# Batch 0 pools q and k on chip from its local tiles, local attention without zero padding, the token rounds cut anew, and the priorities of the order replaced

## The chip, the cores and the metric

The kernel runs on one core of a Trainium2 chip. The metric is the device time of one execution in microseconds. The core has a matrix engine (TensorE, PE in the profile; its weight loads are shown apart as PEld), a vector engine (VectorE, DVE), a scalar engine (ScalarE, ACT), GpSimd (POOL) and SyncE (SP), which here only issues DMAs. Matmul results go to PSUM, which has eight banks of 2 KB per partition.

## The reference

Inputs: q, k, v of shape (4, 8, 576, 64) in fp32, and the weights of two MLPs, w_in (512 x 2048) and w_out (2048 x 512) each, which numpy draws in fp64. The three steps are:

```
q_d, k_d, v_d = mean over each 4 tokens           # 576 -> 144
out_up   = repeat(softmax(q_d k_d^T / 8) v_d, 4)  # "global" attention
out_local = softmax(mask(q k^T / 8)) v            # mask: |i - j| < 4
x = out_up + out_local                            # 2304 tokens x 512
h = x @ moe_w_in;  x = (h * cos(h)) @ moe_w_out
h = x @ moe2_w_in; out = relu(h)**2 @ moe2_w_out
```

## The kernel before

**Tokens and rounds.** The 2304 tokens (4 batches of 576) go through attention and MLP 1 in five rounds, `ROUNDS` (L40): 512, 256, 512, 512, 512 tokens. Weights and activations of the MLPs are split in two fp32r halves, high and low, so each product is three matmuls (`mm3`, L717 to L720). In a round, for each of 16 slices f of the hidden dimension, `mlp_h` makes 128 hidden rows in a PSUM bank with the tag `ps`, ACT and DVE form h cos(h) and its halves, and `mlp_o` adds to four accumulators (tags acc0 to acc3). In round 0 the weights are also converted from fp64 (`convert`, L296 to L308, DVE) and split (L274 on ACT, L277 on DVE); `w_out` goes to DRAM in halves and is loaded again in later rounds. MLP 2 then runs in three blocks of 768 tokens, with seven products for eight (`big_h`, `big_g`, `big_o`), once MLP 1's output is in DRAM.

**Attention units.** For each batch there are four global units (`unit_g`, one pair of heads each, over 144 pooled tokens) and five local units (`unit_l`, tiles of 116 tokens, all eight heads). A round can start when the units that cover its tokens are done (`need`, L1199); the units of the next round are emitted among the work of the current one. Batch 0's units for round 0 are the prologue. Their outputs meet in `xr`, a ring of 640 tokens, from which `split_x` takes the halves xh and xl that `mlp_h` reads.

**A local unit.** The keys of two heads lie in a tile `kz` of 128 partitions in which each head's other 64 partitions are zero, set once by GpSimd (L1251), so that one matmul with 128 rows (q of two heads) and 128 columns gives both heads' scores (L630). A tile has two halves t of 58 queries, which go to output partitions 0 to 57 and 64 to 121. Before them one bf16 matmul of 512 columns writes the mask (L624). Scores of all eight heads fill one bank. `softmax` takes the maximum on DVE (L484); for the first four units (`EXP_SUM`) ACT then takes the exponential group by group with its sum (L498), for the others DVE subtracts (L487), ACT takes one exponential (L492) and DVE sums (L506); DVE divides (L511, L520). PE transposes (L644), ACT copies the two heads into the two partition halves of the zero-padded `pz` (two copies of 64 partitions, L648), PE multiplies with v (L668: 8 matmuls of 128 rows and 116 columns, par choosing the output half), and DVE adds the global part `up_sb` on the way into xr (L694).

**A global unit.** Scores from `qd_sb` (padded per head) and `kd_sb` (L551), the same softmax with ACT's sums, transposes (L567), copies (L570), values with `vd_sb` (L585), and ACT's repeated copy to `up_sb` (L591).

**Pooling.** For batches 1 to 3, GpSimd issues DMAs that add the four phases of q, k, v into `qn_sb`, `kd_sb`, `vd_sb`. For batch 0, q and k are loaded whole a second time (L359), PE sums their phases by identity matmuls (L369), ACT copies (L373, L377), and DVE adds pooled v (L403). Each local tile has its own loads of q, k and v (L441, L445, L448).

**The order.** Every piece is an `op` with an engine, a cost and a key, a due time made of its round and slice. `Plan.order` runs a list schedule over costs and buffer counts: each engine takes what can start first, and among what can start within 0.02 us the smallest key. To the key an entry of the table `OFF` (L53) is added, by the name of the operation and the stage (`STG`) in which its key lies. The resulting order is the program's; on the chip each engine goes through its own part of it, waiting for semaphores. Tags in `IN_TURN` get their buffers in the order of emission. The tag `ps` has four banks. Before the first `mlp_o`, tiny matmuls of zeros (L1240, "idle") fill PE's planned gaps.

Of the kernel before, what the change touches and what calls it, by code (L numbers as in the profile page):

```python
# [7 lines left out]
F32 = mybir.dt.float32  # L8
F32R = mybir.dt.float32r
I32 = mybir.dt.int32  # L10
# [12 lines left out]
QT = 58  # L23
# [10 lines left out]
NORM = 0  # L34
NORM_L = 0
ADD_PE = 0
# [3 lines left out]
ROUNDS = [(0, 512), (512, 256), (768, 512), (1280, 512), (1792, 512)]  # L40
# [16 lines left out]
class Plan:  # L57


    RATE = {"SP": 1.24, "POOL": 2.07}  # L60
    LAT = {"PE": 0.15, "ACT": 0.15, "DVE": 0.15, "SP": 0.0, "POOL": 0.0}

    IN_TURN = ("rawi", "rawo", "w2", "p", "pt", "q", "v", "t", "w1")
# [161 lines left out]
@with_exitstack  # L225
def body(ctx: ExitStack, tc: tile.TileContext, qb, kw, vw, q0, k0, qp, kp, vp, wi, wo, masks, ident, out_t):
# [6 lines left out]
    ATT = ("q", "v", "p", "pt", "mx", "sm")  # L233
# [10 lines left out]
    id16 = const.tile([128, 128], BF16, name="id16")  # L244
    mask16 = const.tile([128, 3, KT], BF16, name="mask16")
    kz = [att.tile([128, 2, 2, PR, KT], F32, name=f"kz{i}") for i in range(2)]
    pz = [att.tile([128, PR, 2, 2, QT], F32, name=f"pz{i}") for i in range(2)]
# [103 lines left out]
    def load_pooled(b, key, after=None):  # L351
        some = [("kd", kd_sb, kp), ("qn", qn_sb, qp), ("vd", vd_sb, vp)]
        if b == 0:
            for c in range(KD):
                for nm, tmp, src, tok in (
                    ("k", xr[:, :, 0:S], k0, [("xr", x) for x in range(XR // 64)]), ("q", up_sb, q0, [("up", x) for x in range(KD)])
                ):
                    def ld(tmp=tmp, src=src, c=c):
                        nc.sync.dma_start(out=tmp[:, c], in_=src[:, c])  # L359

                    op("SP", 0.82, key + c, ld, w=[(nm + "0", c)])

                for nm in ("q", "k"):
                    tile_, src = ("ps", "pool", nm, c), (up_sb[:, c] if nm == "q" else xr[:, c, 0:S])

                    def sums(tile_=tile_, src=src):
                        ps, t = new(tile_, [128, SD], space=PSUM), src.rearrange("p (r g) -> p r g", r=4)
                        for r in range(4):
                            nc.tensor.matmul(ps, id_sb, t[:, r], start=r == 0, stop=r == 3)  # L369

                    def put(nm=nm, tile_=tile_, c=c):
                        if nm == "k":
                            nc.scalar.activation(out=kd_sb[:, c], in_=T[tile_], func=AF.Copy)  # L373
                            return
                        for hh in range(2):
                            pp = slice(64 * hh, 64 * hh + 64)
                            nc.scalar.activation(  # L377
                                out=qd_sb[pp, c, :, hh, :], in_=T[tile_][pp].rearrange("p (t i) -> p t i", i=48),
                                func=AF.Copy,
                            )  # L380

                    op("PE", 1.0, key + c, sums, r=[(nm + "0", c), ("id",)], w=[tile_], new=[tile_])
                    op("ACT", act(SD, 0.05) * (2 if nm == "q" else 1), key + c, put, r=[tile_], w=[(nm + "d", c)])
            for c in range(XR // 64):
                plan.readers[("xr", c)] = sum((plan.writer[("kd", x)] for x in range(KD)), [])
            for c in range(KD):
                plan.readers[("up", c)] = sum((plan.writer[("qd", x)] for x in range(KD)), [])
# [12 lines left out]
            for r in range(1, 4):  # L400
                def add_v(r=r):
                    a = T["w1", "v0", 0][:, 0] if r == 1 else vd_sb
                    nc.vector.tensor_tensor(out=vd_sb, in0=a, in1=T["w1", "v0", r // 2][:, r % 2], op=OP.add)  # L403

                op(
                    "DVE", 1.15, key + 2.5 + 0.5 * r, add_v,
                    r=[("v0", r), ("w1", "v0", r // 2)] + ([("v0", 0)] if r == 1 else []), w=[("vd",)],
                )
            some = []
        else:  # L410
            T_gate = ("gate", b)
            op(
                "POOL", 0.0, key - 0.1, lambda: nc.gpsimd.tensor_copy(out=gate, in_=T[after][0:1, 0:1].bitcast(F32)), r=[after],
                w=[T_gate],
            )
        before = ("gate", b)
        for nm, dst, src in some:
            for r in range(4):
                how = OP.bypass if r == 0 else OP.add
                op(  # L420
                    "POOL", 0.82, key, lambda dst=dst, src=src, r=r, how=how: nc.gpsimd.dma_start(
                        out=dst, in_=src[b, r], accum_op=how), r=[("gate", b)] + ([before] if r == 0 else []),
                    w=([(nm, c) for c in range(KD)] if nm == "kd" else [(nm,)]) + [("pool", b, nm)],
                )
            before = ("pool", b, nm)

    def home(b, d):

        if b == 0 and d in (2, 3):
            return ("ki", "q", d), ("e", "v", d), d  # L430
        return ("q", b, d), ("v", b, d), 0 if (b, d) == (0, 4) else (b * ND + d) % 2

    def keys(kt):
        return kz[kt] if kt < 2 else T["w1", "kz"][:, kt - 2]

    def load_local(b, d, key):
        q, v, kt = home(b, d)
        more = [("w1", "kz")] if kt > 1 else []

        def lq():  # L440
            nc.sync.dma_start(out=new(q, [128, 2, PR, QT]), in_=qb[b, d])  # L441

        def lk(hh):
            pp = slice(64 * hh, 64 * hh + 64)
            nc.sync.dma_start(out=keys(kt)[pp, hh], in_=kw[b, d, pp])  # L445

        def lv():
            nc.sync.dma_start(out=new(v, [128, 2, PR, D]), in_=vw[b, d])  # L448

        if kt == 2:  # L450
            def f_z(i, hh):
                if i == hh == 0:
                    new(("w1", "kz"), [128, 2, 2, 2, PR, KT])
                nc.gpsimd.memset(T["w1", "kz"][64 - 64 * hh:128 - 64 * hh, i, hh], 0.0)

            for i in range(2):
# [929 lines left out]
```

## Time and profile before

| | |
|---|---|
| median of 3 runs | 933.02 us (931.62 to 935.36) |
| profiled execution, span | 930.2 us (the profile gives no other time of it) |
| PE busy | 902.9 us, 97% |
| PE weight loads | 778.6 us, 84% |
| DVE busy | 620.8 us, 67% |
| ACT busy | 428.6 us, 46% |
| POOL busy | 36.1 us, 4% |
| DMA | 204.08 MB, mean 219 GB/s |

The table is part 1 and part 3 of the profile's page. Busy PE time counts from a matmul's start to its modelled end, and matmuls overlap in the pipeline, so 97% says that PE rarely stands idle, not that it runs at its peak. Time that a matmul really takes from the engine is read from the starts of neighbours in the timeline.

### The profile page before, as it was taken

The page shows a single profiled execution, that of the slowest core. Times are in us where ns is not written, and L with a number is a line of the kernel's source. Part 1 is how long each engine was busy: PE and PEld are TensorE (multiplying, and loading weights), DVE is VectorE, ACT ScalarE, POOL GpSimd, SP SyncE. Part 2 cuts the span into 40 slices and gives each one's busy share as a digit, 9 for nine tenths or more (in the row PEclk, how much of TensorE's full clock was granted, in tenths as well). Part 3 has the DMA queues.
Part 4 walks back from the last instruction along what each step waited for, and adds up shares of the span by engine and source line. Part 5 has one row for each costly group of instructions (what it writes and reads, how often), then busy time and mean ns, then how long its engine had stood idle before and what let it go on. Part 6 is the DMA issues. An engine that isn't in the chain of part 4 may idle for free.

```text
span 930.2 us, 14600 instructions
## 1 busy us (share of the span) xinstructions
PE 902.9 (97%) x5456; PEld 778.6 (84%) x5456; DVE 620.8 (67%) x1081; ACT 428.6 (46%) x881; POOL 36.1 (4%) x53
## 2 busy tenths in 40 slices
PE   8899979999899999999999989999999999999998
PEld 8788667898688877888888878998899899999997
DVE  2799999736835359766886789878945453644452
ACT  4966678748656476555675433223311111121111
POOL 2001110110120000000000000000000000000000
PEclk9999999999999999999999999999999999999999
DMA  8848975888756255675888677867776565666643
GB/s 232 283 165 255 300 227 190 258 245 245 207 106 175 84 172 192 246 267 202 282 324 271 238 256 267 302 221 269 229 261 196 177 188 179 209 211 198 182 147 114
DMA packets 79447, 204.08 MB, mean 219 GB/s; under 512 B 9232, under 2 KB 14096, under 8 KB 79376
## 3 DMA queue, kind: packets, MB, share of 16 engines
q1 hardware_dynamic: 75152, 192.51, 62.0%
q0 software_dynamic: 4224, 10.62, 6.2%
q8 instruction: 44, 0.72, 0.3%
q14 instruction: 27, 0.22, 0.1%
HBM read 162.20 MB, written 40.89 MB: 218 GB/s over the span
## 4 chain that ended last, share of the span: by engine, by line
PE 76%; DVE 13%; DMA 6%; ACT 2%; issue 2%; SPq 0%; DVEq 0%
PE acc L718 10%; PE acc L720 10%; PE acc L719 10%; PE pp L718 6%; PE ps L718 6%; PE ps L719 5%; PE ps L720 5%; PE pp L719 5%; PE pp L720 5%; PE acx L1160 2%; PE acx L1158 2%; PE acx L1159 2%; DMA rawo<-in_wo_dram 2%; PE ps L630 2%; DVE wa L303 1%
## 5 line engine op out<-in xcount | busy, mean ns | idle before, releaser
L718 PE MATMUL ps<-xh,w 128*128 128x512 f32 (+1 forms) x320 | 120.5, 377 | 2.5 <-DVE t L758 2.3
L718 PE MATMUL acc<-gh,w 128*128 128x512 f32 (+1 forms) x320 | 120.7, 377 | 1.3 <-ACT w L274 0.6
L720 PE MATMUL acc<-gh,w 128*128 128x512 f32 (+1 forms) x320 | 118.3, 370 | 0.9 <-DVE w L277 0.8
L719 PE MATMUL ps<-xl,w 128*128 128x512 f32 (+1 forms) x320 | 118.1, 369 | 1.1 <-DVE xl L277 1.1
L720 PE MATMUL ps<-xh,w 128*128 128x512 f32 (+1 forms) x320 | 118.2, 369 | 0.5 <-DVE w L277 0.3
L719 PE MATMUL acc<-gl,w 128*128 128x512 f32 (+1 forms) x320 | 118.1, 369 | 0.0
L758 DVE TENSOR_TENSOR t<-t,ps 128x512 f32<-128x512 f32 (+1 forms) x80 | 50.6, 634 | 43.5 <-ACT t L755 43.3
L1090 DVE TENSOR_TENSOR c<-ua,pp 128x384 f32<-128x384 f32 x96 | 52.9, 552 | 34.8 <-PE pp L720 33.2
L277 DVE TENSOR_TENSOR gl<-t,gh 128x512 fp32r<-128x512 f32 (+1 forms) x80 | 50.4, 634 | 34.6 <-ACT gh L274 34.4
L718 PEld LDWEIGHTS ps<-xh,w 128*128 128x128 f32 x320 | 60.3, 188 | 15.2 <-issue 3.0
L718 PEld LDWEIGHTS acc<-gh,w 128*128 128x128 f32 x320 | 60.2, 188 | 13.9 <-issue 1.8
L1128 ACT ACTIVATE xh<-c 128x768 fp32r<-128x768 f32 x32 | 27.1, 846 | 95.5 <-PE acc L720 91.2
L720 PEld LDWEIGHTS acc<-gh,w 128*128 128x128 f32 x320 | 60.3, 188 | 12.7 <-DVE w L277 2.7
L720 PEld LDWEIGHTS ps<-xh,w 128*128 128x128 f32 x320 | 60.3, 188 | 12.0 <-DVE w L277 2.0
L719 PEld LDWEIGHTS ps<-xl,w 128*128 128x128 f32 x320 | 60.3, 189 | 10.9 <-DVE xl L277 1.6
L719 PEld LDWEIGHTS acc<-gl,w 128*128 128x128 f32 x320 | 60.3, 189 | 9.5 <-DVE gl L277 0.5
L1131 DVE TENSOR_TENSOR xl<-c,xh 128x768 fp32r<-128x768 f32 x32 | 30.6, 957 | 56.4 <-ACT xh L1128 56.1
L746 ACT ACTIVATE ki<-ps 128x512 int32<-128x512 f32 (+1 forms) x80 | 44.0, 551 | 49.7 <-PE ps L720 36.8
L274 ACT ACTIVATE gh<-t 128x512 fp32r<-128x512 f32 (+1 forms) x80 | 46.2, 582 | 33.0 <-PE acc L720 23.3
L750 DVE SCALAR_TENSOR_TENSOR t<-ki,ps 128x512 f32<-128x512 int32 (+1 forms) x80 | 50.3, 631 | 16.6 <-ACT ki L746 15.6
L763 ACT ACTIVATE t<-t 128x512 f32<-128x512 f32 (+1 forms) x80 | 46.6, 584 | 26.0 <-DVE t L750 25.3
L1097 ACT ACTIVATE ua<-pp 128x384 f32<-128x384 f32 x24 | 11.7, 489 | 95.5 <-PE pp L720 95.4
(194 smaller groups left out, 2126.8 us busy)
## 6 DMA issues: line engine op xcount, KB each, us to landing
w<-w_dram SPq DMA_DIRECT2D x96, 512.0 KB, 3.4
gh<-w_dram SPq DMA_DIRECT2D x77, 256.0 KB, 2.9
gl<-w_dram SPq DMA_DIRECT2D x77, 256.0 KB, 3.1
rawi<-in_wi_dram SPq DMA_DIRECT2D x32, 512.0 KB, 5.5
rawo<-in_wo_dram SPq DMA_DIRECT2D x32, 512.0 KB, 5.1
w_dram<-w SPq DMA_DIRECT2D x32, 512.0 KB, 4.3
w_dram<-rawo SPq DMA_DIRECT2D x24, 512.0 KB, 4.4
kz<-in_kw_dram SPq DMA_DIRECT2D x36, 128.0 KB, 4.3
```

What stands on the lines that cost most here:

```text
L274: nc.scalar.activation(out=hi(), in_=src(), func=AF.Copy)
L277: nc.vector.tensor_tensor(out=lo(), in0=src(), in1=hi().bitcast(F32), op=OP.subtract)
L718: nc.tensor.matmul(ps, w_hi, r_hi, start=first, stop=False)
L719: nc.tensor.matmul(ps, w_hi, r_lo, start=False, stop=False)
L720: nc.tensor.matmul(ps, w_lo, r_hi, start=False, stop=last)
L746: nc.scalar.activation(out=tt(ki), in_=tt(hp), func=AF.Copy, scale=1.0 / TWO_PI)
L750: nc.vector.scalar_tensor_tensor(out=tt(t), in0=tt(ki), scalar=-TWO_PI, in1=tt(hp), op0=OP.mult, op1=OP.add)
L758: nc.vector.tensor_tensor(out=tt(t), in0=tt(t), in1=tt(hp), op=OP.mult)
L763: "ACT", act(n), key + 0.2, lambda: nc.scalar.activation(out=tt(t), in_=tt(t), func=AF.Abs), w=[t]
L1090: nc.vector.tensor_tensor(out=out(), in0=a(), in1=ps(), op=OP.subtract if sub else OP.add)
L1128: nc.scalar.activation(out=gpart(0, R, f), in_=T[t], func=AF.Copy)
L1131: nc.vector.tensor_tensor(out=gpart(1, R, f), in0=T[t], in1=gpart(0, R, f).bitcast(F32), op=OP.subtract)
```

## The change

- **Local first.** For batch 0 the units are emitted as five local and then four global ones, and round 0 needs all of them. The local output is copied into xr by ACT; the global part is then scaled and added in xr by DVE, two instructions per two heads' pairs.
- **Pooling of batch 0.** The second load of q and k, PE's sums and ACT's copies of them are gone. DVE sums each four tokens of q and k from the local tile (`f_pool`, two reductions per tile); ACT spreads the pooled q. Pooled v is summed by PE (four matmuls of 512 columns for each of two halves), copied by ACT.
- **Local units without padding.** One array `qkv` in DRAM holds a tile's q, k and v; one DMA per tile (two for batch 0, q and k ahead of v) brings them. `kz` and `pz` and their zeroing are gone. Scores are 16 matmuls of 64 rows, 58 outputs and 64 columns: each head's 64 partitions (hh) by each half t. The two heads' results go to two banks. The mask is four bf16 matmuls of 64 rows and 256 columns. Values are 16 matmuls of 64 rows and 58 columns, into two banks. The softmax takes maximum and subtraction per bank; the weights are copied in one instruction of 128 partitions into a `pt` buffer.
- **Global units.** Two units share one product with v and one copy.
- **Constants.** The 16-bit identity and mask come ready-made in one load.
- **Rounds and priorities.** `ROUNDS` becomes 512, 384, 448, 448, 512. The planner's costs of the local products become 0.75 and 0.52 (before 1.25 and 0.95), and `OFF` is replaced by a shorter table.

```diff
+HOMES = ((0, 4),)
+S_PE = 0.75
+PV_PE = 0.52
...
-ROUNDS = [(0, 512), (512, 256), (768, 512), (1280, 512), (1792, 512)]
+ROUNDS = [(0, 512), (512, 384), (896, 448), (1344, 448), (1792, 512)]
...
-        "q": 2, "v": 2, "rawi": 2, "rawo": 2, "wm": 1, "wa": 2, "w2": 3, "p": 3, "pt": 2, "t": 2, "ki": 2,
+        "qkv": 4, "rawi": 2, "rawo": 2, "wm": 1, "wa": 2, "w2": 3, "p": 3, "pt": 2, "t": 2, "ki": 2,
...
+                    for r in range(4):
+                        nc.tensor.matmul(
+                            ps, id_sb[0:SD // 2, 0:SD // 2], T["w1", "v0", r // 2][:, r % 2, kh], start=r == 0, stop=r == 3
+                        )
...
     def load_local(b, d, key):
+        if b:
+            op("SP", 2.08, key, lambda: ld(0, NQ + NK + NV), w=[x, ("v", b, d)], new=[x])
+            return
+        op("SP", 1.36, key, lambda: ld(0, NQ + NK), w=[x], new=[x])
+        op("SP", 0.75, key + 0.5, lambda: ld(NQ + NK, NQ + NK + NV), r=[x], w=[("v", b, d)])
+        n = min(DT, S - DT * d) // 4
+        for nm, dst, lo, m in (("q", qn_sb, 0, DT), ("k", kd_sb, NQ, DT + 6)):
+            def f_pool(dst=dst, lo=lo, m=m, at=3 if nm == "k" else 0):
+                src = T[x][:, lo:lo + PR * m].rearrange("p (r n) -> p r n", r=PR)[:, :, at:at + 4 * n]
+                nc.vector.tensor_reduce(
+                    out=dst[:, :, DT // 4 * d:DT // 4 * d + n], in_=src.rearrange("p r (g f) -> p r g f", f=4), op=OP.add, axis=AX.X
+                )
...
     def unit_g(b, c, key):
+            for hh in range(2):
+                x = xr[:, 2 * j + hh, 0:S].rearrange("p (g r) -> p g r", r=4)
+                nc.vector.scalar_tensor_tensor(out=x, in0=src[:, hh], scalar=0.25, in1=x, op0=OP.mult, op1=OP.add)
...
     def unit_l(b, d, key, on_act):
-            nc.tensor.matmul(
-                ps.rearrange("p r h n -> p (r h) n"), id16, mask16[:, mk:mk + 1, :].to_broadcast([128, 2 * PR, KT]),
-                start=True, stop=False,
-            )
-            for pr in range(PR):
-                for t in range(2):
-                    nc.tensor.matmul(
-                        ps[64 * t:64 * t + QT, pr], T[q][:, t, pr, :], keys(kt)[:, :, t, pr, :], start=False,
-                        stop=(pr == PR - 1),
-                    )
+            for t in range(2):
+                for hh in range(2):
+                    nc.tensor.matmul(
+                        T[s[hh]][half[t]], id16[half[hh], half[hh]],
+                        mask16[half[hh], mk[t], :].unsqueeze(1).to_broadcast([64, PR, KT]), start=True, stop=False,
+                    )
+            for r in range(PR):
+                for t in range(2):
+                    for hh in range(2):
+                        nc.tensor.matmul(
+                            T[s[hh]][64 * t:64 * t + QT, r], q[half[hh], r, QT * t:QT * t + QT],
+                            k[half[hh], r, QT * t:QT * t + KT], start=False,
+                            stop=r == PR - 1,
+                        )
...
+            for j in range(2):
+                for t in range(2):
                     for par in range(2):
+                        for hh in range(2):
+                            nc.tensor.matmul(
+                                T[pv[hh]][half[par], j, t, :], v[half[hh], t, 2 * j + par, :],
+                                weights()[half[hh], 2 * j + par, t, :], start=True, stop=True,
+                            )
...
-        units += [("g", b, p) for p in range(PR)] + [("l", b, d) for d in range(ND)]
+        g, l = [("g", b, p) for p in range(PR)], [("l", b, d) for d in range(ND)]
+        units += g + l if b else l + g
...
-                load_local(u[1], u[2], key - 15.0)
+                load_local(u[1], u[2], key - 15.0 if u[1] else -200.0 + u[2])
...
     op("SP", 0.3, -1.0, lambda: nc.sync.dma_start(out=id_sb, in_=ident), w=[("id",)])
+    op("SP", 0.3, -1.0, lambda: nc.sync.dma_start(out=small_sb, in_=small), w=[("small",)])
```

In the new `OFF` the load of `small` in the first stage has -3512.0 and the loads of local q and k -125.6; the identity's load and pooled v's have no entry (pooled v's keys are -98.5 to -97.0), so the identity's key is -1.0.

## Rows read from the trace of the kernel before

**Rows 1.** The page, parts 1 and 2: busy time, and tenths in 40 slices.
```profile
PE 902.9 (97%) x5456; PEld 778.6 (84%) x5456; DVE 620.8 (67%) x1081; ACT 428.6 (46%) x881; POOL 36.1 (4%) x53
...
PE   8899979999899999999999989999999999999998
```

**Rows 2.** Stretches: length; busy us of PE, PEld, DVE, ACT, POOL; clock, DMA share, GB/s.
```profile
0.00:10.00 10.00, 8.24 (x49) 8.00 (x50) 1.68 (x4) 2.42 (x5) 6.01 (x14) 1.00 0.78 224
10.00:20.00 10.00, 8.38 (x78) 7.77 (x78) 2.25 (x6) 4.99 (x23) 0.00 (x0) 1.00 0.97 245
20.00:30.00 10.00, 9.08 (x118) 7.71 (x118) 8.40 (x16) 9.03 (x43) 0.00 (x0) 1.00 1.02 316
30.00:55.00 25.00, 22.84 (x343) 19.51 (x339) 19.86 (x38) 20.18 (x77) 0.00 (x0) 1.00 0.67 201
55.00:100.00 45.00, 44.57 (x197) 35.32 (x194) 44.72 (x80) 29.72 (x49) 5.45 (x7) 1.00 0.78 252
135.00:172.00 37.00, 36.46 (x270) 26.85 (x269) 35.80 (x77) 28.09 (x58) 1.64 (x3) 1.00 0.70 233
172.00:250.00 78.00, 73.67 (x661) 66.66 (x661) 44.94 (x104) 53.65 (x139) 9.97 (x13) 1.00 0.85 241
250.00:530.00 280.00, 280.00 (x1437) 228.45 (x1436) 189.54 (x334) 173.35 (x314) 7.94 (x10) 1.00 0.63 209
```

**Rows 3.** Timeline of PE: start, us, instruction; the first matmul of round 0.
```profile
54.98 0.48 PE L718 MATMUL ps<-xh,w 128*128 128x512 f32 x1
```

**Rows 4.** Stretch 135 to 172 us for L630, then L668; groups of PE, L585.
```profile
135.00:172.00 37.00, 5.45 (x80) 4.21 (x80) 1.00 0.70 233
...
135.00:172.00 37.00, 1.98 (x32) 1.64 (x32) 1.00 0.70 233
...
L585 PE MATMUL ps<-pt,vd_sb 72*64 72x144 f32 x128 | 10.6, 294 | 0.5 <-DVE sm L511 0.5
```

**Rows 5.** Timeline of PE, 352.1 to 355.6 us: a local unit's products.
```profile
352.13 0.96 PE L668 MATMUL ps<-pz,v 128*64 128x116 f32 x16
353.02 0.66 PE L644 MATMUL ps<-id_sb,p 128*128 128x128 f32 x4
...
354.22 0.39 PE L624 MATMUL ps<-mask,id 128*128 128x512 bf16 x1
354.54 1.09 PE L630 MATMUL ps<-kz,q 128*58 128x128 f32 x16
355.56 0.50 PE L718 MATMUL acc<-gh,w 128*128 128x512 f32 x1
```

**Rows 6.** Timeline of PE, 354.54 to 354.66 us: the first two of them.
```profile
354.54 0.33 PE L630 MATMUL ps<-kz,q 128*58 128x128 f32 x2
```

**Rows 7.** Groups of weight loads: count, busy us, mean ns, idle before.
```profile
L668 PEld LDWEIGHTS ps<-pz,v 128*64 128x64 f32 x288 | 14.4, 136 | 5.6 <-issue 2.3 <-ACT pz L648 2.2 <-ACT up_sb L591 0.4
L719 PEld LDWEIGHTS acc<-gl,w 128*128 128x128 f32 x320 | 60.3, 189 | 9.5 <-DVE gl L277 0.5
```

**Rows 8.** The chain in the prologue (start, us), then groups of ACT and DVE to 55 us.
```profile
25.90 2.49 ACT p L498 x16
...
L648 ACT ACTIVATE pz<-ps 64x464 f32<-64x464 f32 x10 | 5.5, 551 | 3.2 <-PE ps L644 3.1
L591 ACT ACTIVATE up_sb<-ps 128x576 f32<-128x576 f32 x4 | 2.5, 635 | 0.0
L484 DVE TENSOR_REDUCE mx<-s 128x8 f32<-128x512 f32 x5 | 3.4, 686 | 0.8 <-PE s L630 0.8
L694 DVE TENSOR_TENSOR xr<-ps,up_sb 128x464 f32<-128x464 f32 x4 | 2.5, 624 | 0.1
L403 DVE TENSOR_TENSOR vd_sb<-vd_sb,w 72x1024 f32<-72x1024 f32 x2 | 2.4, 1211 | 0.0
```

**Rows 9.** Timeline of SP's queue: the first load of weights.
```profile
22.66 0.33 SPq L292 DMA_DIRECT2D rawi<-in_wi_dram  x1
```

**Rows 10.** Waits of PE, 55 to 250 us: total, times, longest.
```profile
PE ps L644 <- DVE p L520: 2.3, 2, 1.8
```

More of the change, by code (lines that the diff above doesn't have):

```diff
@@ L353, in load_pooled @@
         if b == 0:
[L354 to L379, printed above, removed]
-                            )
[L382 to L387, printed above, removed]
             for r in range(4):
@@ L468, in softmax, with local, ld @@
-    def softmax(u, key, ps, p, view, np_, g, n, scale, on_act):
+    NQ, NK, NV = PR * DT, PR * (DT + 6), 2 * PR * D
+    def local(b, d):
+        return ("qkv", b, d) if (b, d) not in HOMES else ("w1", "qkv", d)
+    def load_local(b, d, key):
+        x = local(b, d)
+        def ld(lo, hi):
+            if lo == 0:
+                new(x, [128, NQ + NK + NV if x[0] == "qkv" else 2048])
+            nc.sync.dma_start(out=T[x][:, lo:hi], in_=qkv[b, d, :, lo:hi])
+        if b:
[10 more added lines that the diff above has]
+                )
+            op("DVE", dve(PR * 4 * n), key + 0.3, f_pool, r=[x], w=[("kd" if nm == "k" else "qn", d)])
@@ L531, in softmax @@
         op("DVE", 0.15 if on_act else 0.3, key + 0.03, f_inv, w=[sm])
-        op("ACT" if norm_act else "DVE", g * act(n, 0.02) if norm_act else dve(g * n), key + 0.04, f_norm, r=[sm], w=[p])
+        op("DVE", dve(g * n), key + 0.04, f_norm, r=[sm], w=[p])
     def unit_g(b, c, key):
         u = ("g", b, c)
-        s, p, pt, pv = ("ps", "s") + u, ("p",) + u, ("pt",) + u, ("ps", "pv") + u
-        if c == 0 and b > 0:
+        s, p, pt = ("ps", "s") + u, ("p",) + u, ("pt",) + u
+        some = [(nm, d) for d in range(ND) for nm in ("qn", "kd")] if b == 0 else [("qn",), ("kd",)]
+        if c == 0:
             def f_q():
@@ L577, in unit_g @@
             op("ACT", act(288), key + 0.1, f_e, r=[tp], w=[pt])
+        if c % 2 == 0:
+            return
+        j, pv = c // 2, ("ps", "pv") + u
+        both = [("pt", "g", b, c - 1), pt]
         def f_pv():
[L580 to L588 removed]
@@ L600, in ring @@
+        op("PE", 1.1, key + 0.2, f_pv, r=both + [("vd",)], w=[pv], new=[pv])
+        if b:
+            op("ACT", act(2 * S), key + 0.2, f_up, r=[pv], w=[("up", 2 * j), ("up", 2 * j + 1)])
+        else:
+            op("DVE", 2 * dve(S), key + 0.2, f_up, r=[pv], w=xtok(0, S))
     def ring(t0, n):
@@ L635, in unit_l @@
-        op(
-            "PE", 1.25, key, f_s, r=[q, ("kz", kt, 0), ("kz", kt, 1), ("id16",), ("mask16",)] + more, w=[bank],
-            new=([s] if b else []) + [p],
+        x, p, tp, pt = local(b, d), ("p",) + u, ("ps", "t") + u, ("pt",) + u
+        s = [("ps", "s", hh) + u for hh in range(2)]
+        pv = [("ps", "pv", hh) + u for hh in range(2)]
+        if b == 0:
+            banks = [("accb", 3), s[1]] if d % 2 else [("accb", 1), ("accb", 2)]
+        else:
+            banks = s
+        mk = [1 - (d == 0), 1 + (d == ND - 1)]
@@ L638, in unit_l @@
+        op(
+            "PE", S_PE, key, f_s, r=[x, ("small",)], w=banks,
+            new=[y for y in banks if y[0] != "accb"] + [p],
         )
-        softmax(u, key, bank, p, lambda: T[s].rearrange("p r h n -> p (r h) n"), 128, 8, KT, 0.125, on_act)
+        softmax(u, key, banks, p, [lambda hh=hh: T[s[hh]] for hh in range(2)], 128, 8, KT, 0.125, on_act)
         def f_t():
             ps = new(tp, [128, PR, 2, 64], space=PSUM)
+            new(pt, [128, 4 * SD])
             for j in range(PR):
@@ new lines, in unit_l, with f_x @@
+        op("PE", PV_PE, key + 0.2, f_pv, r=[x, ("v", b, d), pt], w=pv + xtok(b * S + s0, n), new=pv)
+        for o, c, m in ring(b * S + s0, n):
+            def f_x(o=o, c=c, m=m):
+                for hh in range(2):
+                    dst, src = xr[:, hh:KD:2, c:c + m], T[pv[hh]].rearrange("p j t i -> p j (t i)")[:, :, o:o + m]
+                    if b:
+                        nc.vector.tensor_tensor(
+                            out=dst, in0=src, in1=up_sb[:, hh:KD:2, s0 + o:s0 + o + m], op=OP.add
+                        )
+                    else:
+                        nc.scalar.activation(out=dst, in_=src, func=AF.Copy)
+            op(
+                "DVE" if b else "ACT", 2 * dve(2 * m) if b else 2 * act(2 * m), key + 0.2, f_x,
+                r=pv + ([("up", y) for y in range(KD)] if b else []), w=xtok(b * S + s0 + o, m),
```

279 lines of the change are left out of this document (99 added, 180 removed).

## The prediction

> **What bounds the kernel now.** I read the busy shares first, then the stretches, then the rows behind each term. PE is busy 97% of the 930.2 us span, and its digits are 9 nearly everywhere after the first tenth [rows 1]. The stretches split that: up to 55 us PE does attention of batch 0 and idle fill, and the first matmul of round 0 starts at 54.98 us [rows 2, 3]. From 55 to 100 us DVE is full (44.7 of 45.0) and PE almost (44.6): weight conversion and round 0 run at one pace. From 135 to 172 us both are full again, from 250 to 530 us PE has no gap, and after 570 us its digits stay 9. So a PE microsecond saved after 135 us is a microsecond saved, one before 55 us is worth only what brings 54.98 forward, and DVE decides with it up to 172 us. The granted clock is 1.00 in every stretch (the 2.4 GHz level).
>
> **Local units on PE.** There are 20 (4 batches of 5 tiles), and the five of batch 0 lie before 55 us. Of the 15 others, five scores and two values (80 and 32 instructions, 16 to a unit) run at 135 to 172 us, where PE and DVE are both full [rows 2, 4]; half of their saving is counted, which leaves 13 units' worth. Before, the mask matmul starts at 354.22, the 16 traced instructions of the scores (8 fp32 matmuls, two instructions each) at 354.54, the next matmul at 355.56: 1.34 us. The 16 of weights times values take 352.13 to 353.02: 0.89 us [rows 5]. These rows are pairs: t (or par) selects one of two column halves, and two matmuls of which one alone lasts 0.27 to 0.32 us end within 0.33 us of the first's start, so the halves run side by side; a pair comes every 1.02/8 = 0.13 us counted with both ends, 0.107 of it 128 columns twice at 2.4 GHz [rows 5, 6]. After, each matmul has 64 rows and 64 (58) columns instead of 128 padded rows and 128 (116): twice the instructions, half the columns, four array quarters. If four run side by side, a step of four costs 64 x 2 / 2.4 = 53 ns, which I raise to 60 because each quarter must also load new weights within it: a 64-column load lasts 136 ns, a 128-column one 189, so 64 columns more cost 53 ns [rows 7]. Scores: 8 x 0.06 = 0.48, the mask as four matmuls of 256 columns side by side 0.11, and 0.2 for entering and leaving the split array (the 0.32 of the mask is 0.21 of columns and 0.11 of such a gap): 0.79. Values: 8 x 0.06 + 0.1 = 0.58. Saved: 0.55 + 0.31 = 0.86 us a unit, 13 x 0.86 = **-11**. Bounds: at no charge for weights 1.0 a unit and 15 units, -15; if every instruction costs the mean of today's (1.02/16 = 64 ns), 32 x 64 ns twice is 4.1 + 0.3 against 2.2, +2.2 a unit, +29. I take the value near the lower end, since the two starts lie within 0.06 us of each other.
>
> **Other PE work.** Two global units share one value product: same instructions (128 for all 16 units [rows 4], so 8 to a unit), six switches of the array fewer after batch 0 at about 0.2 us: **-1** (0 to -2). Batch 0's pooled q, k leave PE and its pooled v comes (8 matmuls of 512 columns, 4 passes each: 8 x 0.85 = 6.8 us); PE has fill there, so 0, and where no fill is left up to +3.
>
> **The prologue.** Loads ahead of the identity, in the order of the new keys (mask, four q/k tiles, values, the fifth tile, pooled v): 0.08 + 5 x 0.487 + 5 x 0.262 + 4 x 0.295 + 0.065 = 5.1 MB. At 224, 245, 316 GB/s in the first three ten-microsecond stretches [rows 2] they are in at 21 us. No transpose runs before that: the local units 0 to 2 do scores, maximum and exponentials (three p buffers), the rest waits. DVE, which is idle for 16 of the first 20 us [rows 2], has the ten pooling reductions in them (10 x 0.62 by the 0.686 of 512 elements [rows 8]). From 21 us on ACT is the fullest. From 20 to 55 us it was busy 29.2 us [rows 2]. Of that go five weight copies, as ten become five (2.8), four copies of 0.635 into up (2.5) and three of the four local exponentials, done before 21 us (each 2.49 and two small ones of 0.2: 8.7); five copies into xr come (two pieces each, 3.5), pooled v (1.3), and the two global softmaxes that ran before 20 us (an estimated 1.8 each by 0.31 a group, and 0.4 of copies twice: 4.4) [rows 8]: 24.4 us, to which a wait or two of half a microsecond is added, so round 0's first matmul comes at about 46.5 instead of 54.98. DVE needs as much: from 20 to 55 us it did 28.3; three pooled-v sums (3 x 1.21) and five additions (3.3) go, four scaled additions of 576 come (3.1), two global maxima and norms come from before 20 us (2.5), three local maxima (2.1) go there [rows 8]: 24.9. The first weights land behind 5.6 MB, at about 23 us; before, their load was issued at 22.66 [rows 9]. I take **-8**. Bounds: no dependence bites, ACT starts its last run at 16 us, -13; the chain local, global, final addition stays serial behind the identity, +3.
>
> **Round 0 and the round sizes.** All five rounds hold 2304 columns as before, and a matmul costs columns/2.4 plus the same few ns, so MLP work is 0. Round 1 now needs three local units of batch 1 instead of two, done in round 0 where DVE is full: about 3.4 us more of DVE (maximum 0.75, subtraction 0.75, sum 0.7, norm 0.7, addition 0.6 [rows 8]), of which PE's gap in the sixth slice (116 to 140 us) [rows 1] takes some: **+2** (0 to +4). Round 2 gets one unit fewer to wait for and a longer round 1 (384) to hide it in; 172 to 250 us lacks 4.3 us of PE: **-1** (0 to -3). Split maxima and subtractions add about 0.3 us of DVE a unit, hidden from 250 to 530 us (DVE 190 of 280); uncovered they would be +4. The new priorities reorder everything else; without rows for them I count 0, bounds -4 and +8.
>
> **Sum.** 930.2 - 11 - 1 - 8 + 2 - 1 = 911.2 for the span. The profiled execution's time is its span; the median of the runs, 933.02, lies 2.8 above it, and with that the forecast is **914 us**.
>
> **Rivals.**
> *No fourfold overlap* (the change not doing what it says): row halves take turns. Then a step of four costs two pairs, 32 instructions as long as 16 before, and only the prologue and the rest stay: 914 + 11 = 925. For it: no row here splits rows. Against: column halves do overlap, and the diff gives the row halves different banks.
> *Issue-bound, slower than before:* each of the 32 instructions, or its weight load, takes a turn of its own. Place: the two products of each local unit; price: 64 x s against 2.0 us. With the other 10.8 us saved, the whole is slower from 13 x (64 s - 2.0 + 0.3) > 10.8, s > 40 ns; at today's mean spacing of 64 ns (scores) it is +29 instead of -11, 954; at 50 ns, 942. Against: two starts within 0.06 us [rows 6].
> The Trainium skill ("TensorE: Matmul & The Clock Gate", section "Wait — 56ns, not 53.3ns?") says that matmuls never start closer than about 25 ns, however few columns they have. By that both products take 32 x 25 ns = 0.8 us, a unit saves about 0.2 us, and the time is an estimated 922. The pair of rows 6 contradicts it, at least for two halves.
> *Banks:* a local unit now takes two of the four ps banks for scores and two for values, where it took one each, and each f of a round takes one too. A score bank is held through two maxima and two subtractions (1.5 us and DVE's queue). For it: PE already waited 1.8 us at once for a softmax [rows 10]. Against: from 250 to 530 us nothing waits. At 0.8 us on 13 units 914 + 10 = 924; slower than before only from 1.5 us a unit.
> The Trainium skill ("TensorEngine Tiling (Array Packing)", section "Restrictions and Gotchas") warns of just this, that row tiles must write different banks and so raise the pressure on PSUM.
> *DVE keeps the end of round 0:* the earlier start only moves the wait into 100 to 172 us, the prologue's 8 is lost: 922.
>
> **How the numbers follow.** Forecast 0.58 (own range 904 to 922), no overlap 0.12, banks 0.14, round 0 0.09, issue-bound 0.07. Half a per cent (4.7 us) is about what can be told from no change: faster is below 928.3, slower above 937.7. Faster: all of the forecast, nearly all of no overlap and round 0, and three quarters of banks, less a little for the priorities: 0.82. Slower: issue-bound and the bad end of banks and priorities: 0.11. Same: 0.07. The range takes the forecast with its bounds (-15 instead of -11, -13 instead of -8: 905, with better priorities 901) and the three middle rivals (925 and the priorities' bound): 900 to 932; outside lie the issue-bound case and the tails.
>
> **What would show it.** In the profile after: scores of a local unit, mask to next matmul, 0.8 us instead of 1.34, and values 0.6 instead of 0.89; first matmul of round 0 near 46 us; transposes not before 20 us, with DVE's pooling ahead of them; PE without gaps from 250 to 530 us. Wrong if the 32 instructions last over 1 us, if that first matmul is later than 52 us, or if PE waits for ps banks among local units.

## The result and the profile after

The changed kernel takes **906.88 us** (median, 902.68 to 910.51) against 932.75 (931.62 to 935.36) for the one before on the same chip: ratio 0.9714, 95% interval 0.9678 to 0.9749, some 26 us less. The forecast was 914 in a range of 900 to 932. Direction and the largest cause were right, the sum was 7 us short, and the prologue's mechanism was wrong. All ratios leave out executions more than 1.5% above the fastest of their kernel: here one of a_after's six (1234.33 us) and two of b_rowhalves' six (923.38 and 924.71 us).

The page of the kernel after: busy time, tenths in 40 slices, granted clock. PE's busy time is 17 us less than in [rows 1], its share 1% more; the first two slices have filled from 8 to 9, the sixth (113 to 136 us) stands at 8 where it stood at 7.

```profile
PE 885.9 (98%) x6183; PEld 788.9 (87%) x6183; DVE 620.6 (69%) x1136; ACT 418.8 (46%) x859; POOL 29.0 (3%) x43
...
PE   9999989999999999999999999999999999999998
...
PEclk9999999999999999999999999999999999999999
```

Stretches of the kernel after (columns as in [rows 2]).

```profile
10.00:20.00 10.00, 9.70 (x232) 8.93 (x230) 8.65 (x22) 9.77 (x57) 0.00 (x0) 1.00 1.02 360
20.00:30.00 10.00, 10.00 (x178) 8.00 (x176) 9.40 (x21) 9.01 (x31) 0.00 (x0) 1.00 1.00 351
30.00:48.40 18.40, 18.40 (x250) 14.03 (x249) 17.30 (x34) 12.98 (x42) 0.00 (x0) 1.00 0.75 275
48.40:100.00 51.60, 51.60 (x231) 42.39 (x228) 50.39 (x90) 32.51 (x55) 4.98 (x7) 1.00 0.73 234
100.00:135.00 35.00, 31.70 (x142) 25.17 (x141) 30.32 (x55) 25.53 (x53) 4.76 (x6) 0.95 0.69 195
135.00:172.00 37.00, 34.23 (x473) 28.79 (x473) 30.48 (x80) 23.95 (x58) 2.49 (x4) 0.95 0.71 249
172.00:250.00 78.00, 76.28 (x745) 71.67 (x744) 45.87 (x106) 52.97 (x124) 7.81 (x11) 1.00 0.62 170
250.00:530.00 280.00, 279.49 (x1746) 245.27 (x1745) 201.35 (x388) 171.03 (x319) 8.80 (x11) 1.00 0.70 235
...
118.53:121.94 3.41, 3.41 (x14) 3.08 (x13) 2.40 (x4) 1.60 (x4) 0.83 (x1) 0.50 0.58 180
149.25:152.66 3.41, 3.41 (x11) 2.72 (x11) 2.89 (x10) 2.09 (x3) 0.00 (x0) 0.50 0.77 308
...
530.00:570.00 40.00, 40.00 (x235) 37.55 (x235) 39.52 (x62) 14.66 (x21) 0.00 (x0) 1.00 0.92 325
```

From 20 to 48.4 us DVE is busy 26.7 of 28.4 us, ACT 22.0: DVE is the fuller one. From 100 to 172 us PE has 6.1 us of holes where the kernel before has 7.0 (the first row below, with one of [rows 2]), and two pieces at half clock, which that one doesn't have. The last row above answers to the second one below, where PE stood still for 4.2 us. Both are of the kernel before, with the same columns:

```profile
100.00:135.00 35.00, 28.52 (x133) 21.50 (x132) 31.59 (x59) 24.27 (x58) 5.05 (x6) 1.00 0.85 241
...
530.00:570.00 40.00, 35.82 (x190) 31.24 (x189) 33.80 (x59) 13.45 (x21) 0.00 (x0) 1.00 0.76 266
```

PE's timeline after (start, us, instruction). First line: first matmul of round 0, answering to [rows 3]. Then a local unit's scores and values, answering to [rows 5]; then the scores' row in windows of 0.03, 0.07 and 0.13 us from 333.77, answering to [rows 6].

```profile
48.44 0.48 PE L694 MATMUL ps<-xh,w 128*128 128x512 f32 x1
...
333.64 0.30 PE L617 MATMUL ps<-small_sb 64*64 64x256 bf16 x4
333.77 0.62 PE L624 MATMUL ps<-qkv 64*58 64x64 f32 x32
334.32 0.66 PE L640 MATMUL ps<-id_sb,p 128*128 128x128 f32 x4
...
338.21 0.69 PE L661 MATMUL ps<-pt,qkv 64*64 64x58 f32 x32
338.83 0.47 PE L694 MATMUL acc<-gh,w 128*128 128x448 f32 x1
...
333.77 0.23 PE L624 MATMUL ps<-qkv 64*58 64x64 f32 x4
333.77 0.28 PE L624 MATMUL ps<-qkv 64*58 64x64 f32 x8
333.77 0.34 PE L624 MATMUL ps<-qkv 64*58 64x64 f32 x12
```

Mask to next matmul is 0.68 us (1.34 before), values 0.62 (0.89). The last three lines tell why: four instructions start within 0.03 us, the next four end 0.05 us after them, the next four 0.06 after those. The four transposes at 334.32, of 128 columns each, come about 0.11 us apart one by one, so 64 columns alone are worth an estimated 0.055 us. A step of 56 ns holds four instructions of that length, and by the order of the loops they lie on the four quarters: these do run side by side.

PE's waits after, longest totals (waiting tile and line, releaser: us, times, longest). All but the first lie at 55 to 250 us.

```profile
PE acx L1134 <- DMA w<-w_dram: 3.1, 6, 1.0
PE ps L522 <- DVE t L734: 1.9, 1, 1.9
PE acc L694 <- DMA w<-w_dram: 1.7, 1, 1.7
PE ps L561 <- DVE p L459: 1.6, 1, 1.6
PE ps L538 <- DVE t L734: 1.0, 2, 0.8
PE ps L661 <- ACT pt L646: 0.8, 1, 0.8
```

**Where the 26 us are.** I gave each stretch of PE from one instruction's start to the next to the earlier one's kind of work, with what a 128-row MLP product takes above its usual spacing (0.229 us for 512 columns) as "lost".

| us of PE | before | after | difference |
|---|---|---|---|
| up to round 0's first matmul | 55.0 | 48.4 | -6.6 |
| scores, outside that | 20.1 | 12.1 | -8.0 |
| values, outside that | 15.8 | 9.9 | -5.9 |
| other attention and fill, outside that | 33.0 | 30.9 | -2.1 |
| lost up to the first product of MLP2 | 18.4 | 16.5 | -1.9 |
| lost from there on | 14.0 | 9.9 | -4.1 |
| MLP products | 770.0 | 772.0 | +2.0 |

The rows add to -26.6; the span fell by 26.1 (930.2 to 904.1). Counted in the same way in the two further profiles of the changed kernel (a_after and a_after2), scores and values together take 22.3 and 22.4 us (22.0 in the table), and what is lost behind MLP2's first product about 10 both times. But what is lost before it is about 13 and 18 us, so that row's -1.9 is within what executions of one kernel differ by.

### The profile page after: what moved, and what is told of

The parts are those of the page before. It is cut to its first block, busy times and chain, and to the rows that moved or that the text cites. A ratio compares the mean times of both kernels' runs of the same rounds, so it can differ in the third digit from the quotient of the medians.

```text
span 904.1 us, 15959 instructions
## 1 busy us (share of the span) xinstructions
PE 885.9 (98%) x6183; PEld 788.9 (87%) x6183; DVE 620.6 (69%) x1136; ACT 418.8 (46%) x859; POOL 29.0 (3%) x43
## 4 chain that ended last, share of the span: by engine, by line
PE 69%; DMA 5%; DVE 1%; ACT 1%; issue 0%; SPq 0%; ACTq 0%
PE acc L694 10%; PE acc L695 9%; PE acc L696 9%; PE pp L694 6%; PE pp L696 6%; PE pp L695 6%; PE ps L694 5%; PE ps L696 4%; PE ps L695 4%; DMA w<-w_dram 3%; PE acx L1134 2%; PE acx L1136 2%; PE acx L1135 2%; DMA rawo<-in_wo_dram 1%; DMA x_dram<-e 1%; PE ps L661 1%
## 5 line engine op out<-in xcount | busy, mean ns | idle before, releaser
L694 PE MATMUL acc<-gh,w 128*128 128x512 f32 (+2 forms) x320 | 122.1, 382 | 2.0 <-DMA w<-w_dram 1.7
L694 PE MATMUL ps<-xh,w 128*128 128x512 f32 (+2 forms) x320 | 120.6, 377 | 0.3 <-DVE t L734 0.3
L696 PE MATMUL acc<-gh,w 128*128 128x512 f32 (+2 forms) x320 | 119.0, 372 | 0.4 <-DVE w L276 0.4
L695 PE MATMUL acc<-gl,w 128*128 128x512 f32 (+2 forms) x320 | 118.7, 371 | 0.0
L696 PE MATMUL ps<-xh,w 128*128 128x512 f32 (+2 forms) x320 | 118.4, 370 | 0.0
L695 PE MATMUL ps<-xl,w 128*128 128x512 f32 (+2 forms) x320 | 118.3, 370 | 0.0
L734 DVE TENSOR_TENSOR t<-t,ps 128x512 f32<-128x512 f32 (+2 forms) x80 | 50.6, 632 | 42.2 <-ACT t L731 42.0
L276 DVE TENSOR_TENSOR gl<-t,gh 128x512 fp32r<-128x512 f32 (+2 forms) x80 | 50.6, 634 | 29.5 <-ACT gh L273 28.8
L273 ACT ACTIVATE gh<-t 128x512 fp32r<-128x512 f32 (+2 forms) x80 | 46.6, 585 | 33.0 <-PE acc L696 18.3
L739 ACT ACTIVATE t<-t 128x512 f32<-128x512 f32 (+2 forms) x80 | 46.7, 584 | 32.8 <-DVE t L726 32.5
L722 ACT ACTIVATE ki<-ps 128x512 int32<-128x512 f32 (+2 forms) x80 | 43.0, 548 | 32.2 <-PE ps L696 25.6
L1066 DVE TENSOR_TENSOR ua<-ua,pp 128x384 f32<-128x384 f32 x72 | 39.7, 551 | 24.7 <-PE pp L696 22.8
```

The source lines that it names most:

```text
L273: nc.scalar.activation(out=hi(), in_=src(), func=AF.Copy)
L276: nc.vector.tensor_tensor(out=lo(), in0=src(), in1=hi().bitcast(F32), op=OP.subtract)
L694: nc.tensor.matmul(ps, w_hi, r_hi, start=first, stop=False)
L695: nc.tensor.matmul(ps, w_hi, r_lo, start=False, stop=False)
L696: nc.tensor.matmul(ps, w_lo, r_hi, start=False, stop=last)
L722: nc.scalar.activation(out=tt(ki), in_=tt(hp), func=AF.Copy, scale=1.0 / TWO_PI)
```

## The experiments

Ratios are to the kernel before on the same chip, with 95% intervals. In them the kernel before took 933.7 to 935.1.

**a_after, a_after2: the changed kernel again**, beside the others on two chips.

> The changed kernel again, as the base of this set, with more runs. All theories: ratio to before about 0.971, some 906 us. If stretches of the half granted clock in round 0 cost what they look like (two of 3.4 us each at half speed), runs at a mean clock of 1.000 are 2 to 4 us faster than runs at 0.996.

> The changed kernel again, as the base of this set on this chip: some 906 us.

Measured: 906.55 (ratio 0.9696, 0.9668 to 0.9724) and 907.04 (0.9691, 0.9658 to 0.9723). The executions behind the ratios lie between 901.95 and 910.51 us, so a difference below some 3 us is not told apart here. The profiled executions put the first matmul at 49.8 and 49.5 us. As for the clock: the two executions of the changed kernel at a mean of 1.000 took 902.7 us each and the three at 0.996 took 906.0 to 907.7, a little more than the 2 to 4 us expected. But a_after2's profiled execution has no piece at half clock in its first 904 us and took 907.48, so the pieces alone do not make the spread.

**b_rowhalves: two quarters at a time.** The same instructions, row half after row half.

```diff
-            for r in range(PR):
-                for t in range(2):
-                    for hh in range(2):
+            for hh in range(2):
+                for r in range(PR):
+                    for t in range(2):
```

The values' loops are changed in the same way.

> The loop over the two row halves (hh) is put outermost in the scores and in the values of a local unit: same instructions, same order of everything else, but neighbours now share a row half, so at most two quarters of the array can run side by side. Theory (four quarters overlap): a step of two still takes about 0.055 us, 16 steps instead of 8, so scores +0.45 us and values +0.4 us a unit, 15 units behind the prologue: +10 to +13 us, about 918. Rival (each instruction takes its own turn on the sequencer, overlap is worth nothing): no change, 906 plus or minus 2.

Measured: ratio 0.9753 (0.9722 to 0.9785), a median of 909.77 us over four executions; that is 3.2 us above a_after by the medians (906.55) and 5.4 by the means, and the two intervals just touch. The profile's span is 921.3 us, so only its short rows are read. PE's timeline, a local unit's mask, scores and next matmul, its values, then the scores in windows of 0.03 and 0.07 us:

```profile
349.17 0.30 PE L617 MATMUL ps<-small_sb 64*64 64x256 bf16 x4
349.31 0.90 PE L624 MATMUL ps<-qkv 64*58 64x64 f32 x32
350.13 0.47 PE L694 MATMUL acc<-gh,w 128*128 128x448 f32 x1
...
350.93 0.97 PE L661 MATMUL ps<-pt,qkv 64*64 64x58 f32 x32
...
349.31 0.22 PE L624 MATMUL ps<-qkv 64*58 64x64 f32 x2
349.31 0.28 PE L624 MATMUL ps<-qkv 64*58 64x64 f32 x4
```

Now two start where four did, 0.06 us for each step. Scores and values last 0.28 us longer each: 15 x 0.56 = 8.4 us by the rows, 6.6 by the same count as in the table (28.9 us against 22.3 in a_after), 3 to 5 in the time. The order of the loops, thus the fourfold overlap, is worth some 7 us of PE of the local units' 13.9. It was less than expected since around the middle of the row up to four instructions start together again: the one that signals the end of the first row half is the 21st of 32 to start, so some of the second half start before it (13 steps instead of 16).

**c_vquarter: pooled v from one of four phases.**

```diff
-                    for r in range(4):
+                    for r in range(1):
```

> Batch 0's pooled v is made of one of its four phases only (one matmul of 512 columns for each half instead of four; three phases are left out), in the same order: PE has 5.4 us less in the prologue. Theory (ACT fills the prologue from 7 us on and DVE with it): round 0's first matmul at 47 to 48.4, total within 1.5 us of the changed kernel. Rival (PE's sums stand in the way of transposes and values from 28 to 36 us): first matmul 3 to 5 us earlier, total 3 to 5 us less, about 902.

Measured: 909.46, ratio 0.9743 (0.9716 to 0.977), first matmul at 50.42 us. Three quarters of the pooled v's products on PE gone brings nothing forward. PE waits for ACT's exponentials instead, and a stretch at half clock follows (the longest wait of PE up to 55 us, then the stretch, columns as above):

```profile
PE ps L538 <- ACT p L471: 3.4, 1, 3.4
...
35.18:42.00 6.82, 6.04 (x67) 5.59 (x68) 5.24 (x10) 5.18 (x19) 0.00 (x0) 0.50 0.90 335
```

The last local unit's values start at 38.02 us, against 37.64 to 38.99 in the three profiles of the changed kernel, and from there to the first matmul it takes 12.40 us instead of 10.80, for the half clock. Without that the first matmul would be at an estimated 48.8 us, not 3 to 5 us earlier: the products don't stand in the way.

**d_exptwice: 9.3 us more for ACT in the prologue.**

```diff
-            for i in range(g):
+            for i in [x for x in range(g) for _ in range(2 if n == KT else 1)]:
```

> The exponentials of batch 0's first four local units run twice: 32 more ACT instructions with their sums, 0.29 us each, 9.3 us of ACT before about 30 us, same order. Theory (ACT is what the prologue waits for): first matmul of round 0 7 to 9 us later, near 57, total +6 to +9, about 914. Rival (the loads, or PE's pooled sums behind them, set the end): ACT's time fits beside, first matmul less than 3 us later.

Measured: 918.82, ratio 0.9849 (0.9817 to 0.9881), 12.3 us above a_after. First the timeline, then the stretches:

```profile
61.69 0.48 PE L694 MATMUL ps<-xh,w 128*128 128x512 f32 x1
```

```profile
10.00:20.00 10.00, 5.65 (x112) 5.01 (x109) 3.51 (x9) 9.51 (x54) 0.00 (x0) 0.83 1.00 343
20.00:30.00 10.00, 5.49 (x86) 5.04 (x87) 4.94 (x12) 9.51 (x50) 0.00 (x0) 0.82 0.52 146
30.00:40.00 10.00, 8.69 (x168) 8.04 (x167) 6.47 (x16) 9.45 (x40) 0.00 (x0) 0.84 0.39 116
```

The first matmul came 11.9 us later than a_after's, more than ACT's 9.3, and as much reached the end. With that load ACT sets the pace (9.5 of 10 us) and DVE falls to 3.5 to 6.5; PE idles and drops to half clock in between.

**k_exphalf: 3 us less for ACT there.**

```diff
+                for i in range(0, g, 4):
+                    for h in range(2):
+                        nc.scalar.activation(
+                            out=grp()[:, i + h:i + h + 3:2, :], in_=views[h]()[:, i // 2:i // 2 + 2, :], ...
```

> The first four local units take their exponentials on ACT over two groups at a time with the maximum of the first (maxima and sums of half of the groups are left out): about 0.8 us of ACT less a unit, 3 us before 20 us, same order. Theory (ACT, and nothing earlier, is what the prologue waits for): first matmul of round 0 2 to 3 us earlier, about 46.5. Rival (the run of doubled exponentials only made ACT the bound): no change, 48.4 to 49.8.

Measured: 905.71, ratio 0.9692 (0.9662 to 0.9721); the first matmul came at 52.58 us, later instead of earlier. One wait of PE, and a stretch:

```profile
PE ps L648 <- DMA id_sb<-in_ident_dram: 2.4, 1, 2.4
```

```profile
14.94:21.77 6.83, 5.59 (x68) 5.10 (x69) 2.88 (x7) 3.10 (x17) 0.00 (x0) 0.50 0.96 364
```

Less work for ACT brought nothing forward. But PE waited for the identity here, with half clock from within that wait on, so this run alone does not show that ACT isn't the bound, and the identity had to be tried by itself.

**l_idact: the identity's load out of the way**, on ACT's idle queue at the start.

```diff
-    op("SP", 0.3, -1.0, lambda: nc.sync.dma_start(out=id_sb, in_=ident), w=[("id",)])
+    op("SP", 0.3, -1.0, lambda: nc.scalar.dma_start(out=id_sb, in_=ident), w=[("id",)])
```

> The changed kernel with one load moved: the identity for the transposes is issued on the activation engine's own queue at its start (which idles from 2.0 to 6.8 us) instead of behind eight loads on SyncE's at 4.9. Nothing else changes place on any engine. In the changed kernel it lands 8.4 to 9.6 us after its issue and PE waits up to 1.4 us for it. Theory (the end of the prologue is set by the chain of exponentials and DVE's work, and the identity costs at most its wait): the first local transpose comes about 1.4 us earlier, from 14.2-14.5 to about 13, the first matmul of round 0 stays within 1.5 us (47 to 50), the time within 2 us of the changed kernel's 906.5 to 907.0. Rival (the identity's landing is what the prologue hangs on): first transpose at 11 to 12, first matmul 2.5 us or more earlier than 48.4, time at 904 or less.

Measured: 906.72, ratio 0.9696 (0.9673 to 0.9719), first matmul at 49.35 us. The identity's tile in this kernel (kind, durations, first and last start), and PE's waits up to 55 us:

```profile
L640 PE MATMUL ps<-id_sb,p x8: 272/273/328, 14.4 to 16.0; 128*128 128x128 f32 x8
L1219 ACTq DMA_DIRECT2D id_sb<-in_ident_dram x1: 405/405/405, 0.7 to 0.7; - x1
```

```profile
PE idle L1217 <- issue: 1.7, 2, 1.0
PE s L624 <- DMA qkv<-in_qkv_dram: 1.1, 2, 1.0
PE idle L1217 <- DVE zero L1211: 1.0, 1, 1.0
```

No wait for the identity is left, and the first transpose, the first matmul and the time stand where they were. The rival falls: in the changed kernel the prologue does not hang on the identity. The theory held but for the first transpose, which did not come 1.4 us earlier: ahead of it PE waits 1.1 us for q, k, v tiles and stands idle 1.7 us among its fill, as the lines show.

**e_off0_after, f_off0_before, g_off0_oldrounds: how much is the table of priorities?** It is emptied in the changed kernel, in the kernel before, and in the changed kernel with the old rounds.

```diff
-OFF = {('DVE|convert.f1|wm|wwm', 3): 14455.6, ...
+OFF = {}
```

```diff
-ROUNDS = [(0, 512), (512, 384), (896, 448), (1344, 448), (1792, 512)]
+ROUNDS = [(0, 512), (512, 256), (768, 512), (1280, 512), (1792, 512)]
```

> The changed kernel with an empty table of priorities (OFF), so that the order is the list schedule by due times alone. Together with the next: theory (the gain is in the structure: fewer PE microseconds a local unit and a shorter prologue) is 15 to 25 us faster than the kernel before with an empty table; rival (the gain is the new table, the structure is worth little) within 8 us of it. By itself 30 to 70 us slower than the changed kernel.

> The kernel before with an empty table of priorities. 20 to 50 us slower than the kernel before; the changed kernel with an empty table is 15 to 25 us faster than this (structure), or within 8 us (the table).

> The changed kernel with an empty table and the rounds of before (512, 256, 512, 512, 512). Theory (equal columns, so the sizes are worth only a few us of cover between attention and rounds): within 8 us of the changed kernel with an empty table, either way. Rival (the new sizes carry a large part of the gain): over 10 us slower.

| | priorities | rounds | us | ratio (95%) |
|---|---|---|---|---|
| f_off0_before | empty | old | 976.46 | 1.0456 (1.0433 to 1.0479) |
| g_off0_oldrounds | empty | old | 952.35 | 1.0180 (1.0147 to 1.0212) |
| e_off0_after | empty | new | 958.61 | 1.0259 (1.0234 to 1.0285) |

Without any tuned table the rest of the change brings 24.1 us with the old rounds and 17.9 with the new: most of the gain lies in the structure. Scores and values of all 20 units fall from 46.8 to 31.1 us of PE there (f to e); in g they count 41.4, of which 11.3 are waits behind them. A shorter prologue is hardly part of it: round 0's first matmul lies at 62.1 us in f, 63.7 in g and 58.7 in e. The new rounds cost 6.3 us when the table is empty; that they carry the gain is refuted. The tables are worth 41 us (before, 976.46 to 935.05) and 52 (958.61 to some 906.6, by a_after's ratio).

**i_retuned: the table searched further**, for a plan that stands 2% slower DVE and ACT. **m_idact_retuned** was meant to be that kernel with l_idact's edit, but the load was not moved in what ran: it is i_retuned a second time, and its expectation stays untested.

```diff
-OFF = {('DVE|convert.f1|wm|wwm', 3): 14455.6, ('PE|unit_l.f_t|ps|wps', 4): 240.6, ...
+OFF = {('DVE|convert.f1|wm|wwm', 3): 16536.8, ('PE|unit_l.f_t|ps|wps', 4): 240.7, ...
```

> The changed kernel with a table of priorities searched further so that the planned order stays short when DVE and ACT take 2% more than planned (planned end the same as of the changed kernel). Theory (some 9 us of the changed kernel's time are its order's fragility: waits for banks that DVE frees later than planned, and the half clock after them): 3 to 6 us faster than the changed kernel, about 902, with less lost time in round 0 and fewer stretches at the half clock. Rival (run-to-run spread and the clock are not the order's): 905 to 908.

> The same move of the identity's load onto the activation engine's queue, in the kernel with the searched priorities, whose profile shows PE waiting 2.2 us for that load, half clock at 16.1 to 19.5 us behind the wait, and a first matmul of round 0 at 52.4 us. Theory (the identity costs its wait and the clock behind it): no such wait, no half clock before 20 us, first matmul at 49 to 50.5, time 901.5 to 903 against 904.2. Rival (the chain of exponentials and DVE's work sets the end of the prologue): the wait goes but the first matmul stays within 1 us of 52.4 and the time within 1 us of 904.2.

Measured: 904.19 (903.56 to 904.78), ratio 0.9672 (0.9645 to 0.9699), and 905.46 (900.88 to 909.0), ratio 0.9685 (0.9655 to 0.9714). These are the lowest medians, some 2 us below the changed kernel's, but the intervals overlap: not told apart from it. Fewer pieces at half clock don't show either (two and one, against two, none and none in the three profiles of the changed kernel). The two profiled executions are telling. First matmul at 52.4 and 48.8 us, wait for the identity 2.2 and 0.5 us, yet both spans are 902.5: what came late at the start was made good behind it, where PE lost 12.5 us in rounds 0 to 2 and 7.9 in MLP2 in the one, 14.2 and 9.0 in the other.

## Why the prediction was right, and where not

**Local units: right, a little small.** -11 was forecast, -13.9 measured (scores -8.0, values -5.9), 0.93 us a unit instead of 0.86 and all 15 units instead of 13: half of the seven products at 135 to 172 us was taken off because DVE was full there, but after the change DVE has 6.5 us to spare in that stretch, so their saving can count in full (argued from the row, not tested). A step of four is 56 ns, not 60. The rivals of no fourfold overlap and issue-bound fall by the timeline and by b_rowhalves. (In the issue-bound rival's sum the other savings are 8.0 us, not 10.8, which takes in the 2.8 between span and median: its threshold is 36 ns, and 50 ns would give 944. Nothing else hangs on it.) By the Trainium skill ("TensorE: Matmul & The Clock Gate", section "Wait — 56ns, not 53.3ns?"), whose floor of 25 ns between starts had made an estimated 922, 32 instructions could not start within 0.8 us; here four start within 0.03 us and all 32 end after 0.62, so the trace contradicts it for matmuls of different array quarters. The prediction's own reading of [rows 6], starts within 0.06 us, could not contradict it yet; the trace has these two starts 0.007 us apart.

**Other PE work: right.** -1 was forecast, -2.1 measured with the fill (that the shared value products are the cause was not tested); the pooled v's products were hidden, as c_vquarter shows.

**Prologue: size nearly right, mechanism wrong.** -8 was forecast (first matmul at 46.5), -6.6 measured (48.44). The step that failed is "No transpose runs before that": the prediction put the identity behind 5.1 MB of loads, by their keys, and let it land at 21 us. The identity's tile in the kernel after:

```profile
L640 PE MATMUL ps<-id_sb,p x8: 272/273/328, 14.2 to 15.8; 128*128 128x128 f32 x8
L1219 SPq DMA_DIRECT2D id_sb<-in_ident_dram x1: 927/927/927, 4.9 to 4.9; - x1
...
DMA to landing us min/median/max: 8.4/8.4/8.4
```

It was issued at 4.9 us and landed at 13.3, and the first transpose came at 14.2. In the plan the values' loads wait for the first load to land, whatever their keys, and the identity passed them: eight loads with 3.1 MB stand ahead of it. With that step gone, that the size came near is in part luck. ACT "the fullest" was wrong too: DVE is, from 20 us on, busy 26.7 us to 48.4 where 24.9 to 46.5 was forecast. What sets 48.4 is not settled: more for ACT moves it in full and beyond (d_exptwice), less for ACT (k_exphalf), fewer PE products (c_vquarter) or an early identity (l_idact) don't bring it forward. One thing the profiles do show. From the last local unit's values to the first matmul it takes the same time in the changed kernel and with ACT's doubled exponentials (kernel after, then d_exptwice; their first matmuls are at 48.44 and 61.69):

```profile
37.64 0.69 PE L661 MATMUL ps<-pt,w 64*64 64x58 f32 x32
...
50.89 0.69 PE L661 MATMUL ps<-pt,w 64*64 64x58 f32 x32
```

That is 10.80 us in both, and in the profiles of a_after, a_after2, k_exphalf, l_idact, i_retuned and m_idact_retuned (10.78 to 10.79); c_vquarter's, at half clock, is longer. So the runs moved only what lies ahead of these values. Behind them come the last global units (softmax, transposes, values, additions) and the split of x, with 107 of the zero matmuls in PE's fixed order. That this is a serial chain, the prediction's bound of +3, or that the fill itself holds it up, is not tested; nor did any run take DVE work away, so DVE as the bound is argued, not shown. And of a start some 3 us later the end may see nothing, as i_retuned's two executions show.

**Round 0 and the round sizes: near, by terms that cancel.** +1 in all was forecast, +0.1 measured: PE lost 1.9 us less up to MLP2, which is within the spread of executions, and the products cost 2.0 us more in their new cuts, which the prediction put at 0. The third local unit's cost of DVE time does not show: DVE is less busy at 135 to 172 us than before (30.5 against 35.8 of 37). The banks rival is there in small: waits of ps for L522, L561 and L538 on DVE, 4.5 us in all. PE stands in front of a global unit each time, but in one (L561, 1.6 us) what DVE still has to read is a local unit's scores: the subtractions of L459, of two banks, which run at 147.34 behind a piece of weight conversion. So the prediction's third sign of being wrong, a wait for banks among local units, came in once, for 1.6 us. Two of the waits, 1.9 us at 116.4 to 118.2 and 1.6 at 146.3 to 147.9, are each followed by one of the 3.41 us pieces at half clock, an estimated 1.7 us of columns each; whether that reaches the end is not shown.

**Priorities: 0 taken, and the cover at MLP2 not seen.** From 530 to 570 us the kernel before lost 4.2 us of PE, which now is gone; neither a term nor a rival had it, although the row could have been read. MLP2's first product now runs at 500.88 us, 27 us before the last product of MLP 1 (527.96); before, it ran at 534.15, 6 us before that one (540.16). With empty tables it is 5 to 8 us in all three runs (e, f, g), so the longer overlap comes with the new table. The whole change brings 17.9 us with empty tables on both sides and 26 to 28 with tuned ones. What the new rounds do under a tuned table was not run.

So the 7 us that the forecast is off are, rounded, 3 from the local units, 4 from MLP2, 1 from round 0 with the sizes and 1 from other work, less 1.4 from the prologue.

## What to carry to other kernels

Small matmuls whose operands leave part of the array empty are worth splitting into quarters if the loops put the four quarters next to one another; the same instructions in another order lost 6.6 of 13.9 us of PE, and 3 to 5 us in the time. Where a planner orders the work, read the moment of a load from what it waits for, not from its key. A change that depends on a tuned table is judged with the table emptied on both sides; here that showed 18 us of structure as changed, and 24 without the new sizes. That the sizes pay with their own tuning was not shown.

## What the hardware showed unexpectedly

Four matmul instructions on different quarters start within 0.03 us (0.003 to 0.007 apart), and each step of four takes 0.056 to 0.058 us though each loads its own weights. With the row halves one after the other, matmuls of the second half started before the last ones of the first. PE waits of 1.6 to 2.4 us are followed by a granted clock at half (the 1.2 GHz level) for 3.41 or twice 3.41 us in some executions and not in others. In the first profile of the changed kernel the waits of 1.9 and 1.6 us at 116 to 148 us were followed so; in a_after2's the same two were not, nor were two later ones of 2.2 and 2.1 us. The span with two such pieces was 904.1 us, the two without 900.6 and 905.6, so what the pieces cost at the end is not shown.
